# Reading the moving operand of the B u matmuls in residue order, so that ScalarE reads PSUM in a row

## The chip, the cores and the metric

The kernel runs on one core of one Trainium2 chip. The metric is the device time of one execution in microseconds (us). Engines are named as the profile names them: PE is TensorE's matmuls, PEld its weight loads, DVE is VectorE, ACT is ScalarE, POOL is GpSimd. A matmul has a stationary operand (the weights, loaded from SBUF by PEld) and a moving operand, also read from SBUF; its products land in PSUM.

## The reference, cut to what matters

The input of 2048 tokens x 640 features is normalised, then feeds a diagonal state-space model (S5) and a gated MLP. Only the S5 branch is touched:

```python
xn = _layernorm(x)                                   # (2048, 640)
Bu = jnp.einsum('bld,pd->blp', xn + 0j, B_bar)       # complex, 640 states
for t in range(L):                                   # L = 2048
    h = Lam_bar[None, :] * h + Bu[:, t, :]
y = 2.0 * jnp.einsum('blp,dp->bld', hseq, Cmat).real + xn * Dskip
out = x + y + gated_mlp(xn)                          # gated_mlp: two projections and a spatial matmul
```

## The kernel before

`xnT` holds the normalised tokens transposed in SBUF: 128 partitions of features, and for each of 5 feature blocks 2048 tokens in a row, in bf16 (2 bytes). The scan runs over 256 chunks of 8 tokens, so VectorE wants the B u products by residue: for each `j` in 0..7 all tokens `8 m + j`. Here the matmul reads tokens in a row, and ScalarE sorts them while it copies PSUM (fp32) to SBUF (bf16):

```python
def bu(q, tq):                       # q: 5 blocks of states, tq: 4 blocks of 512 tokens
    b = pair()                       # two PSUM banks: real and imaginary part
    def mm(e):
        for k in range(ND):          # 5 feature blocks
            for ri in range(2):
                r = e.matmul(ps[:, b + ri, :], btv[:, ri, k, q * 128:(q + 1) * 128],
                             xnTv[:, k, tq * 512:(tq + 1) * 512],          # moving, line 682
                             start=(k == 0), stop=(k == ND - 1))
        return r
    pe(mm, ...)
    o = l_m.ap(4096, BF16, q * 8192).rearrange("p (j r t m) -> p r t j m", j=8, r=2, t=4)
    for ri in range(2):              # the copies, line 688 (line 689 after the change)
        act(lambda e, ri=ri: e.copy(o[:, ri, tq], ps[:, b + ri, :].rearrange("p (m j) -> p j m", j=8)), ...)
# ... in between: horner() and scan() of VectorE on these products
def z1_tile(j, half):                # later; tokens of one residue are the STATIONARY operand
    t0 = half * 1024 + j
    b = z_mm(lambda k: xnTv[:, k, t0:t0 + 1017:8], 0, ...)   # weights with a step of 8; line 597
# ... everything else cut
```

That makes 5 x 4 x 10 = 200 B u matmuls of 128x512 (128 rows, 512 moving columns). The order of work on each engine is set when the kernel is built, from fixed costs; the change does not alter those costs.

Of the kernel before, what the change touches and what calls it, by code (L numbers as in the profile page):

```python
# [203 lines left out]
ND = 5  # L204
# [8 lines left out]
def bass_parallel_sum__ssm_conv_s5__mixer_gmlp__prompt_kernel(  # L213
# [17 lines left out]
    with _cl.ExitStack() as _stack, nc.Block() as block:  # L231
# [6 lines left out]
        ps = _stack.enter_context(nc.psum_tensor("ps", [128, 8, 512], FP32))  # L238
# [99 lines left out]
        def bank(b):  # L338
            return ("ps%d" % b, 0, 1)
# [5 lines left out]
        def ca(n, psum=False, ptr=0, acc=0):  # L345
            return (0.055 if psum else 0.095) + n * 0.000833 + 0.093 * ptr + 0.093 * acc
# [6 lines left out]
        def act(f, r, w, occ, name, bias=0.0):  # L353
            return g.add("act", f, r, w, occ, 0.15, name, bias=bias)
# [4 lines left out]
        def pe(f, r, w, occ, name):  # L359
            return g.add("pe", f, r, w, occ, 0.2, name)  # L360
# [16 lines left out]
        xnTv = xnT_m.ap(ND * S).rearrange("p (k t) -> p k t", k=ND)  # L377
# [11 lines left out]
        def xnT_iv(t0, t1):  # L389
            return [xnT_m.iv((k * S + t0 * 128) * 2, (t1 - t0) * 256) for k in range(ND)]  # L390
# [100 lines left out]
        def pair():  # L491
            b = (pslot[0] % 4) * 2
            pslot[0] += 1
            return b
# [180 lines left out]
        def bu(q, tq):  # L675

            b = pair()

            def mm(e):
                for k in range(ND):  # L680
                    for ri in range(2):
                        r = e.matmul(ps[:, b + ri, :], btv[:, ri, k, q * 128:(q + 1) * 128],  # L682
                                     xnTv[:, k, tq * 512:(tq + 1) * 512], start=(k == 0), stop=(k == ND - 1))
                return r
            pe(mm, xnT_iv(tq * 4, tq * 4 + 4) + [bt_m.iv()], [bank(b), bank(b + 1)], 2.16, "bu%d%d" % (q, tq))
            o = l_m.ap(4096, BF16, q * 8192).rearrange("p (j r t m) -> p r t j m", j=8, r=2, t=4)
            for ri in range(2):
                act(lambda e, ri=ri: e.copy(o[:, ri, tq], ps[:, b + ri, :].rearrange("p (m j) -> p j m", j=8)),  # L688
                    [bank(b + ri)], [l_m.iv((q * 8 + j) * 1024 + ri * 512 + tq * 128, 128) for j in range(8)],
                    ca(512, psum=True), "u%d%d%d" % (q, tq, ri))  # L690

# [580 lines left out]
        for q in range(5):  # L1272
            for tq in range(4):
                bu(q, tq)
            if q < 4:
                t_comb(2 * q)
            for j in range(1, 8):
                if q % 2 == 1 or q == 4:
                    if q != 4:
                        horner(q - 1, j)  # L1280
                    horner(q, j)
            if q % 2 == 1 or q == 4:
                if q != 4:
                    scan(q - 1)
                scan(q)
# [122 lines left out]
```

## Time and profile before

| | before |
|---|---|
| time, median of 2 runs | 263.3 us (262.98 to 263.62) |
| span of the profiled run | 261.9 us |
| PE / DVE / ACT busy | 98% / 93% / 68% |
| B u stage, first B u matmul to first z1 matmul | 38.80 to 81.92 us: 43.1 us |
| B u matmuls, start to start | 216 ns |
| granted TensorE clock | 1.00 |

"Start to start" is the distance between successive matmuls. The recorded duration of one matmul (379 ns) is longer than this distance, so neighbouring matmuls overlap, and the distance, not the duration, is the price of a matmul.

The page of the kernel before, its parts on busy tenths in 40 slices (PEclk is the TensorE clock that was granted, in tenths of full speed):

```profile
PE   6999999999999999999999999999999999999995
DVE  4899997999899999999999999999999999999832
PEclk9999999999999999999999999999999999999999
```

PE is at its 9 in nearly every slice and the clock is full. The chain of waits (start us, length us, what), around the B u stage:

```profile
38.80 10.74 PE ps L682 x49
49.59 10.74 PE ps L682 x49
60.38 10.74 PE ps L682 x49
71.18 10.74 PE ps L682 x49
81.92 29.20 PE ps L597 x160
```

Only line 682 and then line 597 stand on the chain there; nothing but TensorE's own speed sets the length of these two stages. (Four of the 200 records are missing from this trace.) The costliest groups of this stage:

```profile
L682 PE MATMUL ps<-arena 128*128 128x512 bf16 x196 | 43.0, 379 | 0.5 <-DMA arena<-in_A_B_im_dram 0.3
L712 DVE SCALAR_TENSOR_TENSOR arena<-arena 128x512 f32<-128x512 bf16 x35 | 25.7, 748 | 0.4 <-ACT arena L688 0.4
L688 ACT CAST arena<-ps 128x512 bf16<-128x512 f32 x40 | 21.2, 598 | 4.6 <-PE ps L682 4.5
```

The columns are busy us, mean ns of one, and idle time before it. The next two lines are weight loads of line 597 (min/median/max ns): first the contiguous ones before the B u stage, then the z1 loads with a step of 8 tokens:

```profile
L597 PEld LDWEIGHTS ps<-arena x120: 96/98/99, 16.2 to 38.0; 128*128 128x128 bf16 x120
...
L597 PEld LDWEIGHTS ps<-arena x158: 140/144/150, 81.9 to 110.6; 128*128 128x128 bf16 x158
```

A step of 8 makes a weight load about 45 ns longer here (144 against 98).

### The profile page before, as it was taken

The numbers are of one execution on the slowest core, as the hardware profiler recorded it, in microseconds if no ns is written. First come the engines' busy times: TensorE is split into PE (matmuls) and PEld (weight loads), VectorE is DVE, ScalarE is ACT, GpSimd is POOL, SyncE is SP. The second block draws the span as 40 slices with busy tenths as digits, with TensorE's granted clock in tenths as the row PEclk, the third lists the DMA queues.
The fourth block names the chain that finished last, engine by engine and source line by source line (L and its number), as shares of the span: only waits on it lengthen the run. The fifth ranks groups of instructions, "written<-read, shape, count | busy, mean of one in ns | idle before, by whom it ended". The sixth has DMA issues, their size and how long they took to land.

```text
span 261.9 us, 4305 instructions
## 1 busy us (share of the span) xinstructions
PE 255.5 (98%) x1487; PEld 151.6 (58%) x1491; DVE 242.3 (93%) x579; ACT 179.1 (68%) x323; POOL 23.0 (9%) x38
## 2 busy tenths in 40 slices
PE   6999999999999999999999999999999999999995
PEld 2555544444446777755555555555557777777773
DVE  4899997999899999999999999999999999999832
ACT  4899999989986545442333676976799889881110
POOL 4255084200000000000000000000000000000000
PEclk9999999999999999999999999999999999999999
DMA  6976899996001855496997858959562566447611
GB/s 185 361 100 131 178 198 227 293 242 123 0 0 38 222 154 163 121 274 125 270 212 161 210 123 197 172 86 270 154 209 45 136 171 154 98 130 205 169 51 50
DMA packets 88243, 41.97 MB, mean 160 GB/s; under 512 B 70975, under 2 KB 88223, under 8 KB 88223
## 3 DMA queue, kind: packets, MB, share of 16 engines
q1 hardware_dynamic: 88078, 41.66, 65.8%
q8 instruction: 11, 0.18, 0.3%
q14 instruction: 10, 0.07, 0.1%
q10 hardware_dynamic: 144, 0.05, 0.1%
HBM read 12.27 MB, written 12.45 MB: 94 GB/s over the span
## 4 chain that ended last, share of the span: by engine, by line
PE 64%; DVE 18%; ACT 7%; DMA 6%; issue 3%; SPq 1%; POOL 1%; DVEq 0%
PE ps L1146 22%; PE ps L682 16%; PE ps L999 12%; PE ps L597 11%; DVE arena L956 3%; DMA arena<-in_A_B_im_dram 2%; DMA g_scratch<-arena 2%; ACT arena L789 2%; DVE arena L734 2%; DVE arena L1039 2%; PE ps L1153 2%; DMA arena<-in_A_x_dram 2%; DVE arena L579 1%; DVE arena L921 1%; DVE arena L919 1%
## 5 line engine op out<-in xcount | busy, mean ns | idle before, releaser
L999 PE MATMUL ps<-arena 128*128 128x432 bf16 x448 | 82.1, 346 | 0.0
L999 PEld LDWEIGHTS ps<-arena 128*128 128x128 bf16 x448 | 43.7, 98 | 38.1 <-ACT arena L1012 0.4
L1146 PE MATMUL ps<-arena 128*128 128x320 bf16 x448 | 64.6, 299 | 0.1
L1146 PEld LDWEIGHTS ps<-arena 128*128 128x128 bf16 x448 | 43.5, 98 | 17.8 <-ACT ps L1175 0.5
L597 PE MATMUL ps<-arena 128*128 128x432 bf16 x280 | 51.6, 346 | 0.0
L789 ACT ACTIVATE arena<-arena 128x512 bf16<-128x512 bf16 x70 | 45.8, 712 | 4.6 <-DVE arena L793 4.5
L597 PEld LDWEIGHTS ps<-arena 128*128 128x128 bf16 x280 | 34.7, 124 | 16.1
L682 PE MATMUL ps<-arena 128*128 128x512 bf16 x196 | 43.0, 379 | 0.5 <-DMA arena<-in_A_B_im_dram 0.3
L1012 ACT ACTIVATE arena<-ps,arena 128x432 f32<-128x432 f32 (+1 forms) x32 | 19.6, 615 | 21.1 <-PE ps L999 17.0
L682 PEld LDWEIGHTS ps<-arena 128*128 128x128 bf16 x200 | 19.5, 98 | 23.9 <-DMA arena<-in_A_B_im_dram 0.5
L712 DVE SCALAR_TENSOR_TENSOR arena<-arena 128x512 f32<-128x512 bf16 x35 | 25.7, 748 | 0.4 <-ACT arena L688 0.4
L1167 DVE TENSOR_TENSOR arena<-ps,arena 128x320 bf16<-128x320 f32 (+1 forms) x40 | 18.5, 482 | 6.8 <-PE ps L1153 5.4
L688 ACT CAST arena<-ps 128x512 bf16<-128x512 f32 x40 | 21.2, 598 | 4.6 <-PE ps L682 4.5
L793 DVE TENSOR_TENSOR arena<-arena 128x1024 bf16<-128x1024 bf16 (+1 forms) x42 | 23.8, 592 | 0.0
L668 ACT ACTIVATE arena<-ps 128x864 bf16<-128x864 f32 x16 | 14.2, 890 | 13.5 <-PE ps L597 13.5
L956 DVE TENSOR_TENSOR arena<-arena 128x1024 bf16<-128x1024 bf16 x32 | 21.3, 684 | 0.5 <-DMA arena<-in_B_w_sp_dram 0.5
L734 DVE TENSOR_TENSOR arena<-arena 128x512 f32<-128x512 f32 (+2 forms) x40 | 21.4, 553 | 0.0
L717 DVE SCALAR_TENSOR_TENSOR arena<-arena 128x256 bf16<-128x256 bf16 (+1 forms) x35 | 16.7, 481 | 0.0
L714 DVE SCALAR_TENSOR_TENSOR arena<-arena 128x256 bf16<-128x256 bf16 (+1 forms) x35 | 16.7, 479 | 0.0
L1113 DVE TENSOR_TENSOR arena<-arena 128x640 bf16<-128x640 bf16 x32 | 15.2, 481 | 0.0
L1175 ACT COPY ps<-ps 128x320 f32<-128x320 f32 x16 | 6.6, 413 | 12.0 <-PE ps L1146 12.0
L1094 DVE TENSOR_TENSOR arena<-arena 128x384 bf16<-128x384 bf16 x32 | 10.9, 350 | 1.2 <-DMA arena<-g_scratch 0.9
(106 smaller groups left out, 253.9 us busy)
## 6 DMA issues: line engine op xcount, KB each, us to landing
g_scratch<-arena SPq DMA_DIRECT2D x16, 224.0 KB, 3.0
z_scratch<-arena SPq DMA_DIRECT2D x16, 216.0 KB, 2.3
arena<-z_scratch SPq DMA_DIRECT2D x8, 432.0 KB, 4.4
arena<-in_A_x_dram SPq DMA_DIRECT2D x16, 160.0 KB, 4.3
base_scratch<-arena SPq DMA_DIRECT2D x16, 160.0 KB, 2.2
arena<-base_scratch SPq DMA_DIRECT2D x16, 160.0 KB, 3.1
out_dram<-arena SPq DMA_DIRECT2D x15, 160.0 KB, 2.8
arena<-in_B_w_in_dram SPq DMA_DIRECT2D x6, 216.0 KB, 4.1
```

What stands on the lines that cost most here:

```text
L597: r = e.matmul(ps[:, b + h, 0:FG], lhs(k), winv[:, k, hcol * FH + h * FG:hcol * FH + (h + 1) * FG], start=(k == 0), stop=(k == ND - 1))
L682: r = e.matmul(ps[:, b + ri, :], btv[:, ri, k, q * 128:(q + 1) * 128], xnTv[:, k, tq * 512:(tq + 1) * 512], start=(k == 0), stop=(k == ND ...
L688: act(lambda e, ri=ri: e.copy(o[:, ri, tq], ps[:, b + ri, :].rearrange("p (m j) -> p j m", j=8)), [bank(b + ri)], [l_m.iv((q * 8 + j) * 10 ...
L712: dve(lambda e: e.scalar_tensor_tensor(tv, prev, lr, cur, op0=ALU.mult, op1=ALU.add), pr + [l_iv(q, j)] + cr, [t.iv()], cd(512) + PTR, nm ...
L734: tt = lambda o, a, b, op: (lambda e: e.tensor_tensor(o, a, b, op))
L789: act(lambda e, pv=pv, hv=hv, lo=lo, sc=sc: e.activation(pv, hv[:, lo:lo + 2, 1:257], ACT.Identity, scale=sc), [h.iv(), Civ(cn)], [m.iv((q ...
L793: dve(lambda e, mv=mv, lq=lq: e.tensor_tensor(lq, lq, mv, ALU.add), li + [m.iv(0, 1024 * n)], li, cd(512 * n, 2), "fix%s%d%d" % (nm, q0, j))
L956: dve(lambda e: e.tensor_tensor(o.ap(1024), x.ap(1024), y.ap(1024), op), [x.iv(), y.iv()], [o.iv()], cd(1024, 2), "%s_%d" % (name, j))
L999: r = e.matmul(ps[:, bk, 0:FG], lv_[:, k, :], rv[k], start=(first and k == 0), stop=(k == 7), skip_group_check=True)
L1012: act(lambda e: e.activation(o, pb(bk), ACT.Identity, bias=bias), [bank(bk)] + bi, [dst], ca(FG, psum=True, ptr=1), name)
L1146: r = e.matmul(ps[:, bk, c0:c1], lf(q), rf(q)[:, c0:c1], start=(first and q == 0), stop=(q == 7), skip_group_check=True)
L1167: dve(lambda e: e.tensor_tensor(o[0][:, c0:c1], ps[:, bk, c0:c1], y[0][:, c0:c1], ALU.add), [bank(bk), y[1]], [o[1]], cd(c1 - c0), "%s_%d" ...
```

## The change

Intent: let TensorE do the sorting by reading the moving operand in residue order (a step of 8 bf16, 16 bytes), so that each PSUM bank arrives sorted and ScalarE reads it in a row.

```diff
-                                     xnTv[:, k, tq * 512:(tq + 1) * 512], start=(k == 0), stop=(k == ND - 1))
+                                     xnTv[:, k, tq * 512:(tq + 1) * 512].rearrange("p (m j) -> p j m", j=8),
+                                     start=(k == 0), stop=(k == ND - 1))
...
-                act(lambda e, ri=ri: e.copy(o[:, ri, tq], ps[:, b + ri, :].rearrange("p (m j) -> p j m", j=8)),
+                act(lambda e, ri=ri: e.copy(o[:, ri, tq], ps[:, b + ri, :].rearrange("p (j m) -> p j m", j=8)),
```

## The prediction

> **What bounds the kernel now.** TensorE. The page shows PE busy 98% of 261.9 us, at full granted clock in every slice. In the B u stage (38.8 to 81.9 us) the chain of waits holds four pieces of 10.74 us of line 682 and almost nothing else: 200 matmuls of 128x512, start to start about 43.1/200 = 216 ns (each is recorded as 379 ns because they overlap). The 160 z1 matmuls follow at once (29.2 us, 182.5 ns each). ScalarE is no bound: the timeline shows it waiting about 1.08 us for TensorE every 2.16 us at 76 to 82 us.
>
> **What the change removes.** The PSUM read of the 40 copies becomes contiguous; their SBUF write stays 8 runs of 64. Contiguous ScalarE PSUM copies here take 413 ns at 320 columns and 511 at 432, so about 581 at 512 (my estimate). The strided copies take 564 to 645, mean 598. Gain about 0.6 us of ScalarE in total, off the critical path: nothing.
>
> **What it adds.** No instruction, same schedule. But each moving operand is read with a step of 8 bf16 = 16 bytes. [...]
>
> This trace has one sign: the z1 weight loads (line 597, after 81.9 us) read the same tensor with the same step and take 142 to 144 ns, against 98 for line 597's contiguous loads before 38.8 us: 45 ns for 128 columns. There they hide behind 182.5 ns matmuls[...]. How it carries over is my main doubt:
> - one column at a time: 45/128 = 0.35 ns a column, so 216 + 180 = about 395 ns a matmul, +36 us;
> - half rate: about 430 ns, +43 us;
> - [...]
>
> **How much lands.** Almost all. TensorE is back to back through this stage and the next; DVE works on B u results, so it is delayed with it, and only catches up some backlog later (PE loses about 2 us at 142 to 195 us; perhaps 1 comes back).
>
> **Prediction.** 306 us (263.3 + 43), 8 in 10: 285 to 398. Faster by over 2%: 0.02; within 2%: 0.14; slower by over 2%: 0.84.
>
> **What would show it.** The B u matmuls' start-to-start time: 216 ns unchanged (wrong), 390 to 430 (half rate), 850 to 900 (quarter rate). The B u stage grows from 43 us by what the span grows, within 3 us. Copies at about 580 ns; ScalarE's and DVE's idle time on line 682 grows by tens of us. The z1, spatial and output stages keep their lengths; z1's weight loads stay at 142.
>
> **What would make it wrong.** [...] a step of exactly 16 bytes is free: then 263 us. [...] Or the delayed DVE work gives back more than I allow.

One of the three ways to carry the 45 ns over came to about 900 ns a matmul and +130 us; it is the "quarter rate" above, and the upper end of the range, 398, covers it (263.3 + 130). The central sum is 263.3 + 43 = 306 us. Its half rate is an estimate, twice the 216 ns of the trace (200 x 216 ns more are 43.2 us); that the factor is two was not shown.

## The result, and the profile after

| | before | after |
|---|---|---|
| time, median of 2 runs | 263.3 us | 402.03 us (402.00 to 402.07) |
| span of the profiled run | 261.9 us | 400.3 us |
| B u matmuls, start to start | 216 ns | 900 ns |
| B u stage | 43.1 us | 180.2 us |
| z1 stage (160 matmuls) | 29.20 us | 30.47 us |
| from there to the end | 150.8 us | 150.6 us |
| ScalarE copy of 512 columns, mean | 598 ns | 588 ns |
| granted clock, mean | 1.00 | 0.777 |

The ratio of times is 1.5255, 95% interval 1.5205 to 1.5306.

The page after, the same parts as shown of before:

```profile
PE   7999999999999999999999999999999999999996
DVE  5999601600032303264992700799999999999962
PEclk9999755555555555555555999999999999999999
```

DVE, busy nearly all the time before, now has holes from slice 5 to slice 19 and in slices 22, 24 and 25. Up to slice 22 its long waits are for ScalarE, whose copies wait for line 682; the hole in slices 24 and 25 is a wait of 25.1 us for matmuls after z1 (line 1000). The granted clock is halved through most of the B u stage. The chain of waits after:

```profile
39.02 180.16 PE ps L682 x200
219.19 30.47 PE ps L597 x160
249.66 74.47 PE ps L1000 x408
```

The four pieces of line 682 of before have become one of 180.16 us for 200 matmuls, 900 ns each. The difference of the spans, 138.4 us, adds up from the chain's boundaries: 137.0 in the B u stage, 1.3 in z1, 0.2 before the stage, and -0.1 after it. The groups after:

```profile
L682 PE MATMUL ps<-arena 128*128 128x512 bf16 x200 | 180.2, 1078 | 0.1
L689 ACT CAST arena<-ps 128x512 bf16<-128x512 f32 x40 | 21.5, 588 | 140.1 <-PE ps L682 140.1
L713 DVE SCALAR_TENSOR_TENSOR arena<-arena 128x512 f32<-128x512 bf16 x35 | 25.5, 744 | 42.5 <-ACT arena L689 42.5
```

The copies wait 140.1 us for line 682 (4.5 before), and VectorE's line 713 (712 before), which works on their products, waits 42.5 us for the copies (0.4 before). These waits follow from the slow matmuls; they do not cause them.

Since the clock is halved, the first question is whether the clock is the cause. Windows of the kernel after (us, then busy us and instructions of each engine, PEclk, DMA share, GB/s):

```profile
core 0: us, PE busy (x) PEld busy (x) DVE busy (x) ACT busy (x) POOL busy (x), PEclk, DMA share, GB/s
38.80:44.00 5.20, 5.11 (x7) 0.69 (x7) 5.20 (x18) 2.96 (x8) 2.28 (x2) 1.00 1.06 263
44.00:60.00 16.00, 16.00 (x19) 2.27 (x18) 2.29 (x7) 3.97 (x8) 1.83 (x1) 0.50 0.92 253
60.00:219.00 159.00, 159.00 (x177) 22.20 (x176) 58.78 (x126) 33.41 (x50) 1.82 (x1) 0.50 0.02 4
219.00:221.00 2.00, 2.00 (x7) 0.98 (x6) 0.67 (x1) 1.76 (x3) 0.00 (x0) 0.50 0.20 44
221.00:223.00 2.00, 2.00 (x10) 1.34 (x9) 2.00 (x6) 1.28 (x2) 0.00 (x0) 0.84 0.60 120
```

and its weight loads, one for each matmul, first in the stretch of full clock and then in that of half clock (first and last start us at the end):

```profile
L682 PEld LDWEIGHTS ps<-arena x5: 116/116/116, 39.9 to 43.5; 128*128 128x128 bf16 x5
...
L682 PEld LDWEIGHTS ps<-arena x189: 126/126/126, 48.0 to 217.2; 128*128 128x128 bf16 x189
```

Five loads from 39.9 to 43.5 us are 0.90 us apart, at a granted clock of 1.00. The 189 loads from 48.0 to 217.2 us are 169.2/188 = 0.90 us apart, at 0.50. So the matmuls were already this slow before the clock fell. The DMA share falls from 1.06 to 0.02 and VectorE's work changes as well, and the 0.90 us stays: no contention with other engines or transfers either.

### The profile page after: what moved, and what is told of

Read it like the earlier page. It is cut to its first block, busy times and chain, and to the rows that moved or that the text cites. A ratio compares the mean times of both kernels' runs of the same rounds, so it can differ in the third digit from the quotient of the medians. Undisturbed runs are those within 1.5% of the kernel's fastest.

```text
span 400.3 us, 4309 instructions
## 1 busy us (share of the span) xinstructions
PE 394.6 (99%) x1491; PEld 157.7 (39%) x1491; DVE 242.8 (61%) x579; ACT 180.0 (45%) x323; POOL 23.0 (6%) x38
## 4 chain that ended last, share of the span: by engine, by line
PE 87%; DVE 4%; ACT 4%; DMA 3%; SPq 1%; POOL 1%; issue 0%; DVEq 0%
PE ps L682 45%; PE ps L1000 19%; PE ps L1147 15%; PE ps L597 8%; DMA arena<-in_A_B_im_dram 1%; DMA arena<-in_A_x_dram 1%; PE ps L1154 1%; DVE arena L579 1%; ACT arena L790 1%; ACT arena L623 1%; DVE arena L545 1%; ACT arena L520 1%; ACT arena L522 1%; SPq L371 1%; DVE arena L581 1%; POOL arena L540 1%
## 5 line engine op out<-in xcount | busy, mean ns | idle before, releaser
L682 PE MATMUL ps<-arena 128*128 128x512 bf16 x200 | 180.2, 1078 | 0.1
L682 PEld LDWEIGHTS ps<-arena 128*128 128x128 bf16 x200 | 25.0, 125 | 153.8 <-issue 153.3
L689 ACT CAST arena<-ps 128x512 bf16<-128x512 f32 x40 | 21.5, 588 | 140.1 <-PE ps L682 140.1
L1000 PEld LDWEIGHTS ps<-arena 128*128 128x128 bf16 x448 | 43.8, 98 | 38.0 <-ACT arena L1013 0.3
L713 DVE SCALAR_TENSOR_TENSOR arena<-arena 128x512 f32<-128x512 bf16 x35 | 25.5, 744 | 42.5 <-ACT arena L689 42.5
L1147 PEld LDWEIGHTS ps<-arena 128*128 128x128 bf16 x448 | 43.6, 98 | 17.7 <-ACT ps L1176 0.5
L597 PEld LDWEIGHTS ps<-arena 128*128 128x128 bf16 x280 | 34.9, 125 | 18.5 <-issue 2.9
L957 DVE TENSOR_TENSOR arena<-arena 128x1024 bf16<-128x1024 bf16 x32 | 21.3, 683 | 25.6 <-PE ps L1000 25.1
L936 DVE TENSOR_TENSOR arena<-arena 128x864 bf16<-128x864 bf16 x16 | 9.0, 602 | 41.4 <-ACT arena L652 41.4
```

Source lines behind the costliest of these rows:

```text
L597: r = e.matmul(ps[:, b + h, 0:FG], lhs(k), winv[:, k, hcol * FH + h * FG:hcol * FH + (h + 1) * FG], start=(k == 0), stop=(k == ND - 1))
L713: dve(lambda e: e.scalar_tensor_tensor(tv, prev, lr, cur, op0=ALU.mult, op1=ALU.add), pr + [l_iv(q, j)] + cr, [t.iv()], cd(512) + PTR, nm ...
L957: dve(lambda e: e.tensor_tensor(o.ap(1024), x.ap(1024), y.ap(1024), op), [x.iv(), y.iv()], [o.iv()], cd(1024, 2), "%s_%d" % (name, j))
L1000: r = e.matmul(ps[:, bk, 0:FG], lv_[:, k, :], rv[k], start=(first and k == 0), stop=(k == 7), skip_group_check=True)
L1147: r = e.matmul(ps[:, bk, c0:c1], lf(q), rf(q)[:, c0:c1], start=(first and q == 0), stop=(q == 7), skip_group_check=True)
```

## The experiments

Nine kernels ran. Single looks are of unknown state (one run each), but their start-to-start times and stages are read from one trace. The correctness check cannot see a wrong token order in the S5 branch. It is no proof of the order in any of these runs; where a result is called right below, that follows from the indices.

**The theory (L)**, formed from the result: TensorE's read of SBUF costs 1.76 ns (900/512) for each visit to a 16-byte line, however many successive elements it takes from the line in that visit; a matmul takes that or 216 ns, whichever is longer. A line here is an aligned stretch of 16 bytes in a partition; that this is the unit was a supposition, which e3, e4 and e5 test. The rivals are named in the expectations.

### e1_act_alone: only ScalarE's half

```diff
-  e.copy(o[:, ri, tq], ps[:, b + ri, :].rearrange("p (m j) -> p j m", j=8))
+  e.copy(o[:, ri, tq], ps[:, b + ri, :].rearrange("p (j m) -> p j m", j=8))
```

> Only the ScalarE half of the change (PSUM read in a row), tokens read in their stored order, so the result is wrong on purpose. Theory (all of the loss comes from the moving operand, ScalarE is off the critical path): same time as before within 0.3%, copies 585 to 592 ns as in the changed kernel, against 598 mean before. Rival (the contiguous copies shift the order of work on ScalarE and DVE and carry part of the loss or a gain): more than 0.5% away from before.

Measured in 6 runs: 263.76 us against 263.68 of before in the same rounds; ratio 1.0005, 95% interval 0.9986 to 1.0024. The copies (ScalarE, min/median/max ns), first of the kernel before, then of this one:

```profile
L688 ACT CAST arena<-ps x40: 564/592/645, 41.2 to 82.4; 128x512 bf16<-128x512 f32 x40
```

```profile
L688 ACT CAST arena<-ps x40: 565/592/647, 41.7 to 82.7; 128x512 bf16<-128x512 f32 x40
```

The time is as theory L expected. The copies did not get shorter: reading in a row left them at a median of 592 ns, exactly the median before (means 600 and 598 ns). So ScalarE's half of the change saves nothing, even on ScalarE.

### e2_pe_alone: only TensorE's half

```diff
-  xnTv[:, k, tq * 512:(tq + 1) * 512], start=(k == 0), ...
+  xnTv[:, k, tq * 512:(tq + 1) * 512].rearrange("p (m j) -> p j m", j=8), start=(k == 0), ...
```

> Only the TensorE half (moving operand with a step of eight), ScalarE reads PSUM with a step as before, result wrong on purpose. Theory: 402 us, start to start 901 ns in B u, equal to the changed kernel within 0.5%. Rival (the two parts interact): more than 1% away from 402.

Measured: 401.86 us (2 runs), ratio 1.524, interval 1.5204 to 1.5275; start to start 900 ns. The whole loss lies in the moving operand. Its copies, which read PSUM with the old step, and below them those of the kernel after, in a row:

```profile
L688 ACT CAST arena<-ps x40: 586/588/591, 48.5 to 220.0; 128x512 bf16<-128x512 f32 x40
```

```profile
L689 ACT CAST arena<-ps x40: 585/588/592, 48.2 to 219.7; 128x512 bf16<-128x512 f32 x40
```

588 ns with a step here, 588 ns in a row in the kernel after; 592 ns with a step before, 592 in a row in e1. In these four kernels the 4 ns go with the rest of the kernel, not with ScalarE's step.

### e3_steps: five steps in one kernel

The five blocks `q` read with steps of 1, 2, 4, 8 and 16 elements within each 512 tokens; ScalarE's pattern undoes the order.

```diff
-  xnTv[:, k, tq * 512:(tq + 1) * 512]
+  xnTv[:, k, tq * 512:(tq + 1) * 512].rearrange("p (a s) -> p s a", s=(1, 2, 4, 8, 16)[q])
```

> Right result. The five groups of 40 B u matmuls read with steps of 1, 2, 4, 8 and 16 elements (2, 4, 8, 16, 32 bytes). Theory L (the port takes 1.76 ns for each visit to a 16-byte line, however many elements it takes from it in a row): start to start 216, 225, 450, 901, 901 ns, total about 328 us. Rival A (any element not next to the one before costs 1.76 ns): 216, 901, 901, 901, 901, about 374 us. [...] Rival C (8-byte granule): 216, 450, 901, 901, 901. Rival D (only the 16-byte step collides with itself): 216, 216, 216, 901, 216.

Measured: 329.51 us. The weight loads of the five groups; there is one for each matmul, so (last start - first start)/(count - 1) is the start-to-start time:

```profile
L690 PEld LDWEIGHTS ps<-arena x35: 98/98/98, 39.1 to 46.4; 128*128 128x128 bf16 x35
...
L690 PEld LDWEIGHTS ps<-arena x38: 95/96/97, 47.1 to 55.4; 128*128 128x128 bf16 x38
...
L690 PEld LDWEIGHTS ps<-arena x38: 96/115/115, 56.1 to 72.8; 128*128 128x128 bf16 x38
...
L690 PEld LDWEIGHTS ps<-arena x38: 116/123/123, 74.1 to 107.4; 128*128 128x128 bf16 x38
...
L690 PEld LDWEIGHTS ps<-arena x38: 123/126/129, 110.1 to 144.1; 128*128 128x128 bf16 x38
```

| step | 1 | 2 | 4 | 8 | 16 |
|---|---|---|---|---|---|
| bytes | 2 | 4 | 8 | 16 | 32 |
| visits to lines, for 512 elements | 64 | 128 | 256 | 512 | 512 |
| theory L, ns | 216 | 225 | 450 | 901 | 901 |
| measured, median of the distances, ns | 216 | 225 | 451 | 900 | 918 |

Rivals A, C and D each miss at least one of these by a factor of 2 or more.

### e4_runs: runs of neighbours

```diff
+  # q = 0..4, of each 512 tokens
+  "p (h l e) -> p l h e" (h=2, e=8)    # whole lines, hopping 512 bytes
+  "p (m u e) -> p u m e" (u=2, e=4)    # runs of 4
+  "p (m u e) -> p u m e" (u=4, e=2)    # runs of 2, 16 bytes apart
+  "p (n u e) -> p u n e" (u=2, e=2)    # runs of 2, 8 bytes apart
+  "p (a s) -> p s a"     (s=64)        # single elements, 128 bytes apart
```

> Right result. Moving reads in runs: group 0 whole lines of 8 elements, hopping 512 bytes between lines; group 1 runs of 4 with a hop of 16 bytes; group 2 runs of 2 with a hop of 16 bytes; group 3 runs of 2 with a hop of 8 bytes; group 4 single elements with a step of 128 bytes. Theory L (1.76 ns a line visit): 216, 225, 450, 225, 901 ns, total about 301 us. Rival C (8-byte granule): group 3 450 ns, the rest as L. Rival A for single elements only (a pair next to each other is enough): 216, 216, 216, 216, 901. Rival E (the two-level access pattern is what costs): group 0 slow too.

Measured: 300.37 us, and in order:

```profile
L690 PEld LDWEIGHTS ps<-arena x37: 98/98/98, 38.5 to 46.3; 128*128 128x128 bf16 x37
...
L690 PEld LDWEIGHTS ps<-arena x38: 95/96/96, 47.0 to 55.3; 128*128 128x128 bf16 x38
...
L690 PEld LDWEIGHTS ps<-arena x38: 115/115/115, 56.2 to 72.8; 128*128 128x128 bf16 x38
...
L690 PEld LDWEIGHTS ps<-arena x38: 95/96/96, 74.0 to 82.3; 128*128 128x128 bf16 x38
...
L690 PEld LDWEIGHTS ps<-arena x38: 114/124/124, 83.6 to 115.4; 128*128 128x128 bf16 x38
```

The medians of the distances are 216, 225, 451, 225 and 860 ns. A two-level pattern costs nothing (group 0, 216 ns), a run of 4 elements costs what theory L says (225), and groups 2 and 3, both in pairs, differ as the number of lines does (451 and 225). A pair is not enough, and the unit is not 8 bytes.

### e5_odd_steps: steps that are no power of two

```diff
-  xnTv[:, k, tq * 512:(tq + 1) * 512]
+  xnT_m.ap(ND * S)[:, k * 128:k * 128 + 511 * STEP[q] + 1:STEP[q]]     # STEP = (3, 5, 7, 9, 12)
```

> Wrong result on purpose: plain one-level reads with steps of 3, 5, 7, 9 and 12 elements (6, 10, 14, 18, 24 bytes) in the five groups. Theory L (1.76 ns a line visit; 512 elements touch 192, 320, 448, 512, 512 lines): 338, 563, 788, 901, 901 ns start to start, total about 360 us. Rival D (a 16-byte step is special, a bank collision): all near 216. Rival A (any element not next to the one before): all 901.

Measured: 362.7 us. The weight loads of the steps 3, 5 and 7:

```profile
L683 PEld LDWEIGHTS ps<-arena x37: 100/101/101, 38.7 to 50.9; 128*128 128x128 bf16 x37
...
L683 PEld LDWEIGHTS ps<-arena x37: 115/117/117, 52.5 to 72.8; 128*128 128x128 bf16 x37
...
L683 PEld LDWEIGHTS ps<-arena x38: 115/122/122, 75.3 to 104.4; 128*128 128x128 bf16 x38
```

Start to start (medians) 338, 563, 787, 927 and 893 ns, against 338, 563, 788, 901 and 901 of theory L. A step of 16 bytes is not special: 10 and 14 bytes took 563 and 787 ns, so rival D is out. Up to a step of 8 elements (e3, e4 and this run) the fit is within 1 ns. At one visit for each element with larger steps (9, 12 and 16 elements, and 64 in e4) the time varies from 860 to 927 ns, where theory L gives 901 throughout. It is not the clock: at the same granted clock of 0.50 the distance was 860 ns in e4 (90 to 115 us), 918 in e3 (110 to 144 us) and 927 in e5 (107 to 141 us). Why it varies stays open.

### e7_weights: the same rule on the weight side

```diff
-  b = z_mm(lambda k: xnTv[:, k, t0:t0 + 1017:8], ...)
+  M, st = ((128, 1), (128, 2), (128, 4), (128, 8), (128, 16), (64, 1), (64, 8), (96, 8))[j]
+  b = z_mm(lambda k: xnTv[:, k, j:j + (M - 1) * st + 1:st], ..., M)    # writes ps[0:M] only
```

> Wrong result on purpose: the z1 weight loads with (columns, step): (128,1), (128,2), (128,4), (128,8), (128,16), (64,1), (64,8), (96,8) by output row group. [...] Rival (one stream for all loads, 0.35 ns extra a column at step 8): the 64-column load with step 8 under 125 ns and the 96-column one under 135. Total within 2% of before either way, unless a weight load exceeds the 182.5 ns of the matmul that hides it.

Measured: 264.01 us, result wrong. The weight loads for (128,1), (128,4), (128,8), (64,1), (64,8), (96,8):

```profile
L597 PEld LDWEIGHTS ps<-arena x14: 97/98/98, 82.2 to 84.6; 128*128 128x128 bf16 x14
...
L597 PEld LDWEIGHTS ps<-arena x16: 112/113/115, 89.3 to 92.1; 128*128 128x128 bf16 x16
...
L597 PEld LDWEIGHTS ps<-arena x16: 140/145/150, 93.0 to 95.7; 128*128 128x128 bf16 x16
...
L597 PEld LDWEIGHTS ps<-arena x16: 111/111/111, 100.2 to 103.0; 128*64 128x64 bf16 x16
...
L597 PEld LDWEIGHTS ps<-arena x16: 192/193/194, 103.9 to 106.6; 128*64 128x64 bf16 x16
...
L597 PEld LDWEIGHTS ps<-arena x16: 250/251/252, 107.6 to 110.3; 128*96 128x96 bf16 x16
```

(128,2) took 98 and (128,16) took 144 ns. With a step of 8, 64 columns take longer (193) than 128 columns (145), and even in a row they do (111 against 98); the rival, with under 125 and under 135 ns for 64 and 96 columns at a step of 8, is out. From 64 to 96 columns the load grows by 58 ns, 1.8 ns a column, close to the 1.76 ns of a line visit. On the line through these two loads (77 ns and 1.8 ns a column, my estimate) 128 columns would take about 309 ns; 145 ns is the time of 38 columns. So a load of all 128 columns does not pay for its columns one after the other at that price. How it avoids this was not shown.

The matmuls above these loads kept a distance of about 0.18 us (16 loads of 96 columns, one for each matmul, start from 107.6 to 110.3 us; 182.5 ns before), apart from single longer distances where the column count changed: even the loads of 251 ns, longer than a matmul's 182.5, left no mark on the total. They too started about 0.18 us apart, so they overlapped; the recorded duration of a load, like that of a matmul, is not its price.

### e6_psum_steps and e6b_psum_all: sorting on the PSUM side

The same intent can be met without touching the read: read in a row, and let the matmul write PSUM in residue order. First in mixed groups, then in all of them:

```diff
-  r = e.matmul(ps[:, b + ri, :], btv...
+  r = e.matmul(ps[:, b + ri, :].rearrange("p (j m) -> p m j", j=8), btv...
-  e.copy(o[:, ri, tq], ps[:, b + ri, :].rearrange("p (m j) -> p j m", j=8))
+  e.copy(o[:, ri, tq], ps[:, b + ri, :].rearrange("p (j m) -> p j m", j=8))
```

> Right result. The other way to the same intent: the moving operand is read in a row and the matmul writes PSUM with a step. Groups: 0 in a row; 1 pairs of columns 256 apart; 2 and 3 residue order, step of 64 fp32, so that ScalarE reads in a row; 4 step of 8. [...] 430 ns or more in groups 1 to 4, total over 300 us. Rival (accumulation writes in PSUM cost the same in any order): 216 ns in all groups, 263 us.

Measured: 298.01 us; 216 ns in group 0 and 429 ns in each of the other four, whatever the step (a little under the 430 ns and 300 us that I had set as bounds). For these single fp32 elements the size is a factor of 2; e8 below shows a step that costs nothing.

> Right result; the same intent reached on the other side in all five groups: tokens read in a row, PSUM written in residue order, ScalarE reads PSUM in a row. From the earlier run's 429 ns for stepped PSUM writes: 200 x (429 - 216) = 42.7 us, so 306 us within 1%, the granted clock stays 1.00 and the z1 matmuls take 29.2 us. Rival (part of the PSUM groups' cost came from the mixed orders or from ScalarE's reads): under 300 or over 312 us.

Measured: 305.95 us (4 runs, 305.82 to 306.32), ratio 1.1597, interval 1.1565 to 1.1628; 429 ns in all groups, granted clock 1.00, z1 in 29.20 us. Its chain of waits:

```profile
38.77 85.83 PE ps L682 x200
124.60 29.20 PE ps L597 x160
```

This does the whole of what the change wanted for less than a third of the loss, and is still slower than the kernel before.

### e8_mixed: lines that are straddled, PSUM pairs, both costs at once

```diff
+  # group: PSUM order written            order read
+  0:       in a row                      "p (m u e) -> p u m e" (u=2, e=4), starting 2 elements into a line
+  1:       "p (u m e) -> p m u e" (e=2)  in a row
+  2:       "p (u m e) -> p m u e" (e=4)  in a row
+  3:       "p (m j) -> p j m"            "p (m j) -> p j m" (j=8)
+  4:       "p (u e m) -> p u m e"        "p (m u e) -> p u m e" (u=4, e=2)
```

> Result wrong in group 0 only. Group 0: runs of 4 that start 2 elements into a line, so that half of the runs straddle a line: theory L (visits to aligned 16-byte lines, 192 of them) 338 ns; rival (a cost per jump, 128 of them) 225; rival (8-byte granule) 450. Groups 1 and 2: read in a row, PSUM written in adjacent pairs and in runs of 4 fp32: if PSUM's cost is per 8-byte visit 216 ns both; if per jump or per element off the row 429 in group 1. Group 3: step of 8 on the read and the same step on the PSUM write: 900 if the two costs overlap, about 1110 if they add. Group 4: pairs read (450 alone) with single PSUM writes (429 alone): 450 if they overlap, about 660 if they add.

Measured: 301.02 us; medians of 227, 216, 216, 900 and 451 ns.

Group 0 missed the 338 I wrote for theory L. My count, redone after the result: only 64 of the 128 runs straddle, and each of these ends in the line in which the next one begins, so there are 64 + 65 = 129 visits, not 192, and 129 visits at 1.76 ns are 227 ns (my estimate). Counted so, the group no longer tells L from a cost per jump (e3 does: with a step of 2 all 512 elements jump, and it took 225); it only excludes the 8-byte unit. In groups 1 and 2 adjacent pairs of fp32 (8 bytes), and runs of 4, cost nothing: 216 ns, against 429 for single ones in e6. In groups 3 and 4 the costs of reading and of writing overlap and the longer one counts: 900 ns from 900 (read) and 429 (write), 451 from 451 and 429. And group 3, as a window:

```profile
core 0: us, PE busy (x) PEld busy (x) DVE busy (x) ACT busy (x) POOL busy (x), PEclk, DMA share, GB/s
64.88:99.20 34.32, 34.32 (x40) 4.49 (x39) 15.19 (x30) 9.51 (x14) 0.00 (x0) 1.00 0.00 0
```

40 matmuls of 900 ns ran here for 34 us at a granted clock of 1.00. That is the clock rival tested a second way: full clock, same 900 ns.

No experiment points to a version that beats the kernel before: ScalarE's copies cost the same either way (592 ns in e1 and before), and both full sorts in TensorE cost time on the engine that bounds (900 ns a matmul on the read, 429 on the PSUM write, against 216).

## Why the prediction was right or wrong

- **What bounds: right.** TensorE's chain, back to back through the stage; every us added to it arrived in the total (137.0 of 138.4).
- **What is saved: right in effect, wrong in detail.** I estimated the copies at 581 ns in a row, from other shapes, and a gain off the critical path. They gained nothing: 592 against 592 (e1), 588 against 588 (after and e2).
- **Direction: right.** With each element in a new 16-byte line a matmul took 900 ns instead of 216, and nothing hid it: all 180.16 us of the 200 matmuls stand in the chain of waits. The way to no loss that the prediction kept open, a free step of 16 bytes, did not hold. The trace before did show the 144 against 98 ns of the weight loads.
- **Size: wrong, and this is the step that failed.** The prediction had three ways to carry the 45 ns of the weight load over and took the second, "half rate: about 430 ns, +43 us". Measured: 900 ns, +137 us. Nearest was the third, with about 900 ns. I had even costed it low: 200 x (900 - 216) ns is 136.8 us, not +130 or so, and with 137 the range would have had to reach beyond 400 us, not to 398. That it came to 900 does not show its ground. The price measured is 1.76 ns a visit, which takes the place of the 216 ns instead of adding to it (e3: 128 visits take 225 ns). The first way spread the 45 ns over 128 columns, 0.35 ns each; e7 shows that this is not what a column costs: 1.8 ns from 64 to 96 columns with a step of 8. e3 to e5 show the price per line.
- **"The B u stage grows by what the span grows, within 3 us": right** (137.0 and 138.4). **"The z1, spatial and output stages keep their lengths": right but for z1**, which took 1.3 us more. Its first part ran at half clock: PEclk is 0.50 from 219 to 221 us and 0.84 in the next 2 us. Seven of its matmuls started about 360 ns apart there, against 183 afterwards, which is 1.2 us. After e6b, where the clock never fell, z1 took 29.20 us. I had not foreseen the fall of the clock.
- **"Perhaps 1 us comes back" from VectorE's backlog: not seen.** The stages after z1 took 150.6 us against 150.8.

## What to carry to other kernels

Count the 16-byte lines that a moving operand visits: here each visit cost 1.76 ns (1.68 to 1.81 with steps above 8), so a bf16 read needed at least four elements from a line before it moved on (225 ns against 216 in a row, but 451 with two and 900 with one). If data must be sorted, do it where it is hidden or free: in the weight load (in e7 loads of up to 251 ns left the total at 264.01 us), or in ScalarE's read of PSUM, which here cost the same with a step as in a row (592 and 592 ns, 588 and 588). When a trace shows the cost of a pattern on one port, first find out how that cost grows with the number of columns (here 193 ns for 64, 251 for 96, but 145 for 128), before you scale it to another.

## What the runs show of the clock, and leave open

Matmuls followed each other with no recorded gap in the kernel after (PE busy 16.00 us of the 16.00 from 44 to 60 us), and the granted clock still fell to 0.50 about 5 us after the start of the 900 ns matmuls. In e3, e4 and e5 it fell 3 to 4 us after the first of 900, 860 and 787 ns (my estimate, from its mean of 0.61, 0.87 and 0.63 in the window from 74 to 90 us). It did not fall at 429 ns (e6b, 1.00 over the run), at 451 ns (e3 and e4, 1.00 from 64 to 74 us) or at 563 ns (e5, 1.00 from 55 to 64 us), nor at 900 ns when PSUM was written with a step too (e8, group 3, 1.00). What makes the clock fall, and why that group kept it, stays open.
